# Summing the middle unit's outputs in SBUF, with one quarter of the weights' sums moved to VectorE

## The chip, the cores and the metric

The kernel runs on one core of one Trainium2 chip. The metric is the device time of one execution in microseconds; of several executions the median is given.

## The reference

Chunked attention is followed by a layer norm and a two-layer network with a residual sum:

```python
# q, k, v: (8, 8, 576, 64); chunks of 64 tokens, each attends to itself
scores = scale * q_c @ k_c.T
attn = softmax(scores)                      # the row's maximum subtracted first
x = (attn @ v_c)  -> (8, 576, 512)          # heads side by side
xn = (x - mean) / sqrt(var + 1e-6) * g_ln
out = x + max(xn @ w_ch1, 0) @ w_ch2        # 512 -> 2048 -> 512
```

The 8 x 576 = 4608 tokens are 18 pairs of 256 rows ("pair" in the code), and two pairs make a tile, so there are 9 tiles. The hidden layer of 2048 is worked on in 16 parts of 128, numbered f.

## The kernel before

**Stages.** The first three tiles (numbers 0 to 2 in the code) are computed directly, while the weights come in and are converted from 64-bit input; a matmul is done as three, from a high and a low half of each operand (`hh` and `hl` for the hidden layer, `wh` and `wl` for the weights). The third of them is called tile 3 below. The six tiles that are left form three units (u = 0, 1, 2) of two tiles, four pairs each. A unit's first product (line 1035) uses seven products in place of eight, on sums and differences of quarters of the operands; so does the second product of units 1 and 2 (line 946, class `double`). Unit 0's second product is a plain one (line 1161). Unit 1 is the middle unit, unit 2 the last one (`tail`).

**What feeds the units.** The sums of the first layer's weights (`wa`) are made by `prepare`, those of the second layer (`wb`) by `mix`, from the converted weights, on GpSimd while tile 3 is computed (`mix_early` for p = 4 to 7) and on VectorE in unit 0 (`mix_late` for p = 0 to 3); p counts eight parts of two f each. All go to DRAM and come back through a ring of six places in SBUF, which SyncE's queue fills in order (`Ring.fetch`: `wa`, `wb` and `w2d`, the plain second layer). `attention` of the next unit's pairs is woven into the running unit, at cost units that count TensorE's work (one for a matmul of 512 columns). `BEGINS[u][n]` says where pair n of the next unit begins, `PAIR_STEPS[u][n]` at which offsets its steps are played. Every pair writes its x to its rows of `out` in DRAM (`spill`, line 262) and sends a turned copy of its normalised rows to the tile `rows` (line 482). `combine` makes the operands `xc` of the next unit from `rows`, in two halves whose places are in `HALVES`: the casts are on ScalarE (line 799), the low halves on GpSimd for the first half and on VectorE for the second (line 803), and the differences on VectorE (line 806), in place, so that a difference waits for the low halves that still read the tile.

**The double product.** The seven products of line 946 are named by `DOWNS = "4126573"`. Each has eight items p, and an item is 12 matmuls of 256 columns. Items are worked on in pairs, and a pair takes one ring place. The operand of an item is split ahead of time: `high` on ScalarE (line 888) and `low` on VectorE (lines 893 and 897), into five buffers in turn, so ScalarE can write one when TensorE has left it. The functions `mix_2`, `mix_3` and `mix_4` (lines 1057, 1065 and 1062) make the next products' operands in place on VectorE. `plan` lists all of this with a due time in items, counted from the product's begin, and `advance` plays what is due behind each group of six matmuls. Two accumulator tiles of two banks each, `a` and `c`, are used in turn, each for eight items.

**What becomes of the sums.** A finished accumulator belongs to one or two quarters of the output: n is the tile of the unit, half is the half of the columns, i one of the tile's two pairs. In the last unit, x is brought back into SBUF (`bring_back`) and VectorE adds the accumulator to it (`gather`, line 911), then it is stored. In the middle unit ScalarE copies the accumulator to SBUF (`copy_out`, line 922) and GpSimd's queue issues DMAs that add the copy to the rows of `out` in DRAM (`add_out`, line 928).

**The order.** Everything is recorded under a manual schedule: each engine executes its instructions in the order in which the code issues them, and waits for what they need. What stands behind a waiting instruction on the same engine or queue waits too. The first three tiles are played from strings and tables of letters; `THIRD` is the table for tile 3: `T` and `V` are `mix_early`, `Q` is `combine`'s second half for unit 0, `H` the attention of a pair. `REST` plays the last steps of `Q` in unit 0. The tag of a tile names the memory that it takes over (`w12` was part 12 of the weights); `keep` has four buffers for x, and the pool `work` two.

Of the kernel before, what the change touches and what calls it, by code (L numbers as in the profile page):

```python
# [17 lines left out]
P = 128  # L18
# [27 lines left out]
    11: "HGGPTT", 12: "GTTT", 13: "GTT", 14: "GGHP", 15: "GHPT", 16: "GHPTT", 17: "GPTVV", 18: "HHGPVV", 19: "HGPTT",  # L46
    20: "HGPVTT", 21: "HHPVV", 22: "HPVT", 23: "TT", 24: "HT", 25: "H", 26: "QQ", 27: "QR", 28: "Q", 29: "QXXN",
    30: "QQR", 31: "Q",
# [3 lines left out]
BEGINS = ((8, 122, 236, 350), (4, 92, 152, 240))  # L52
STEPS = (0, 5, 9, 14, 20, 31, 42, 53, 61, 67, 72, 77, 85, 90, 97, 104, 111, 118, 125)
ACROSS = (0, 5, 9, 14, 20, 31, 42, 53, 61, 67, 72, 77, 110, 116, 123, 130, 136, 142, 148)
BY_TENSOR = (0, 6, 11, 18, 28, 32, 36, 44, 50, 56, 64, 69, 77, 84, 90, 96, 102)
AT_END = (0, 6, 11, 18, 28, 32, 36, 44, 50, 88, 98, 103, 110, 117, 123, 129, 135)
PAIR_STEPS = ((STEPS, STEPS, ACROSS, STEPS), (STEPS, BY_TENSOR, STEPS, AT_END))
HALVES = (((426, 8), (562, 12)), ((500, 7.5), (600, 11)))
SECOND_HALF = 528
MIXING = (1, 4, 13, 16, 24, 37, 41, 47)  # L60
# [45 lines left out]
def chunk_attention_ffn(ctx: ExitStack, tc: tile.TileContext, qkv, v01, g, w, out):  # L106
# [723 lines left out]
    class double:  # L830

        def __init__(self, u, hu, mix_2, mix_3, mix_4):
            self.hu, self.first, self.tail = hu, 2 * LEAD + 4 * u, u == UNITS - 1
            self.items = [(x, p) for x in DOWNS for p in range(NF // 2)]
            self.pools, self.split, self.ys, self.xs, self.plan = {}, {}, {}, {}, []
            for i in range(len(self.items)):
                if not self.tail:
                    at = (-5, -4.5, -1.7, -1, -0.3)[i] if i < 5 else i - 4
                elif i < 8:
                    at = (-5, -4.5, -3.5, -3, -2.5, -2, -0.9, 0.2)[i]  # L840
                else:
                    at = i - (7 if i < LONG else 6 if i < LONG + 5 else 4)
                self.plan += [(at, self.high, i), (at + 0.6, self.low, i)]
            for p in range(NF // 2):
                if self.tail:
                    self.plan += [(2.2 + 1.2 * p, mix_2, p), (13 + 1.8 * p, mix_4, p), (22 + 1.6 * p, mix_3, p)]
# [57 lines left out]
        def gather(self, bank, n, half):  # L904
            last = (n, half) == (0, 1)
            cols = slice(half * PAIR, (half + 1) * PAIR)
            for i in range(2):
                y = self.ys[bank][i].rearrange("p (j d) -> p j d", j=2)
                x = self.xs[n][:, i, :, cols]
                for j in [slice(k, k + 1) for k in range(2)] if last else [slice(0, 2)]:  # L910
                    nc.vector.tensor_tensor(out=x[:, j], in0=y[:, j], in1=x[:, j], op=ALU.add)
                    if last:
                        self.store(n, i, j.start, cols)
            if (n, half) == (0, 0) and bank == "c":
                for i in range(2):
                    for j in range(2):
                        self.store(n, i, j, cols)

        def copy_out(self, bank):
            self.staged = keep.tile([P, 2, DM], F32, name="x")  # L920
            for i in range(2):
                nc.scalar.copy(self.staged[:, i], self.ys[bank][i])

        def add_out(self, bank, places):
            for n, half in places:
                cols = slice(half * PAIR, (half + 1) * PAIR)
                for i in range(2):
                    nc.gpsimd.dma_start(
                        spilled[self.first + 2 * n + i][:, :, cols],
                        self.staged[:, i].rearrange("p (j d) -> p j d", j=2), accum_op=ALU.add,  # L930
                    )
# [67 lines left out]
    def mix_early(pool, tag, ps):  # L999
        for p in ps:  # L1000
# [3 lines left out]
                lambda k: [x[:, DM:].bitcast(F32) for x in weights(2 * p + k)], nc.gpsimd,  # L1004
# [250 lines left out]
    with tc.manual_schedule():  # L1255
# [4 lines left out]
            G=tiles[3].attention(1), H=tiles[4].attention(1, True, pt_raw=True), S=prepare(), R=start_ring(), T=mix_early(raws, "raw", (4, 5, 7)), V=mix_early(const, "w7", (6,)), P=combine(0, 0), Q=combine(0, 1),  # L1260
# [15 lines left out]
        side = [(at, now["Q"]) for at in REST]  # L1276
# [56 lines left out]
```

## Time and profile before

| | us |
|---|---|
| median of three executions | 840.89 |
| lowest and highest of them | 838.8, 842.84 |
| the profiled execution's own time | 837.73 |
| its span in the trace | 835.6 |
| TensorE busy in the span | 820.4 |
| VectorE busy | 591.5 |
| ScalarE busy | 331.5 |
| GpSimd busy | 197.7 |

All times in the trace count from the begin of the span. The stages, as TensorE's lines in the chain that ended last show them: the first three tiles until 326 us, unit 0 from 326 to about 500, unit 1's first product until 588.9 and its second until 675.2, unit 2's first until 751.4 and its second until the end. In the rows, PE is TensorE, DVE VectorE, ACT ScalarE, POOL GpSimd and SPq SyncE's queue of DMAs; L946 is line 946 of the kernel before. A timeline row gives the start, the busy time, the engine, the line, the operation, output and input by the program's names, how many instructions were merged into the row, and in brackets the idle time ahead of it and what ended it. A row of grouped instructions gives the count, the busy time, the mean of one in ns, and the idle time ahead. A row of DMA issues gives the count, the size of one, and the median time from the issue to the landing.

### The profile page before, as it was taken

What the parts mean: (1) busy time and instruction counts of PE and PEld (TensorE: products, weight loads), DVE (VectorE), ACT (ScalarE), POOL (GpSimd) and SP (SyncE); (2) the same over time, 40 slices, a digit from 0 to 9 for tenths busy, and PEclk for the clock granted to TensorE, in tenths of its full rate; (3) what the DMA queues carried; (4) which work ended last, traced back from release to release, by engine and by line L of the source; (5) the groups of instructions that cost most, each with busy time, mean ns of one, the idle gap of its engine ahead of it and who ended that gap; (6) DMA issues with size and microseconds to landing.
All of it is one profiled execution on the core that took longest, in us unless ns stands there. A gap on an engine that the chain in (4) does not pass through costs nothing.

```text
span 835.6 us, 16319 instructions
## 1 busy us (share of the span) xinstructions
PE 820.4 (98%) x6442; PEld 702.1 (84%) x6442; DVE 591.5 (71%) x959; ACT 331.5 (40%) x523; POOL 197.7 (24%) x180
## 2 busy tenths in 40 slices
PE   7999999999999999999999999999998999999998
PEld 4888888888888878888888888788998988889998
DVE  6999966787655945876787858796875932248854
ACT  4776431122322332323334443334554632255432
POOL 0110006463755893000015010000014611000000
PEclk9999999999999999999999999999999999999999
DMA  9997407948883239777867999687898898768673
GB/s 360 336 280 223 167 35 252 322 159 289 319 278 124 102 143 337 257 273 248 275 225 221 363 312 325 224 272 239 253 263 200 216 227 223 206 203 277 208 217 102
DMA packets 108092, 199.54 MB, mean 239 GB/s; under 512 B 9328, under 2 KB 66160, under 8 KB 106096
## 3 DMA queue, kind: packets, MB, share of 16 engines
q1 hardware_dynamic: 101216, 187.48, 65.8%
q0 software_dynamic: 6800, 11.01, 8.2%
q8 instruction: 51, 0.84, 0.4%
q14 instruction: 25, 0.20, 0.1%
HBM read 138.69 MB, written 50.86 MB: 227 GB/s over the span
## 4 chain that ended last, share of the span: by engine, by line
PE 87%; POOL 5%; DVE 3%; DMA 2%; ACT 1%; issue 1%; SPq 1%; DVEq 0%; POOLq 0%; ACTq 0%
PE y L1035 25%; PE y L946 19%; PE h L563 13%; PE y L587 13%; PE y L1161 8%; PE h L1161 3%; PE s L307 2%; POOL mixed L985 2%; POOL mixed L978 1%; PE h L407 1%; DMA k_t<-qkv 1%; DMA wa<-parts 1%; POOL xc L803 1%; DVE pt_sb L378 1%; PE s L407 1%
## 5 line engine op out<-in xcount | busy, mean ns | idle before, releaser
L1035 PE MATMUL y<-xc,ring 128*128 128x512 f32 x1008 | 233.7, 391 | 0.0
L1035 PEld LDWEIGHTS y<-xc,ring 128*128 128x128 f32 x1008 | 187.9, 188 | 39.5
L563 PE MATMUL h<-xth,wp 128*128 128x512 f32 (+1 forms) x432 | 129.3, 370 | 0.0
L946 PE MATMUL y<-ring,hx 128*128 128x256 f32 x876 | 110.2, 285 | 4.0 <-DVE hx L897 4.0
L946 PEld LDWEIGHTS y<-ring,hx 128*128 128x128 f32 x876 | 108.1, 194 | 4.2 <-DVE hx L897 4.2
L1044 DVE TENSOR_TENSOR hu<-y,snap 128x512 f32<-128x512 f32 x72 | 49.2, 687 | 75.5 <-ACT snap L1041 42.1
L587 PE MATMUL y<-wp,hh 128*128 128x512 f32 x376 | 96.2, 394 | 0.0
L563 PEld LDWEIGHTS h<-xth,wp 128*128 128x128 f32 x432 | 78.2, 188 | 14.1
L587 PEld LDWEIGHTS y<-wp,hh 128*128 128x128 f32 x376 | 69.1, 188 | 13.9
L563 PE MATMUL h<-xtl,wp 128*128 128x512 f32 (+1 forms) x216 | 78.2, 367 | 0.0
L577 DVE SCALAR_TENSOR_TENSOR hl<-h,hh 128x512 fp32r<-128x512 f32 (+1 forms) x53 | 33.1, 629 | 62.4 <-ACT hh L576 62.2
L1041 ACT COPY snap<-y 128x512 f32<-128x512 f32 x72 | 42.1, 586 | 80.5 <-PE y L1035 80.4
L576 ACT ACTIVATE hh<-h 128x512 fp32r<-128x512 f32 (+1 forms) x53 | 28.6, 546 | 106.2 <-PE h L563 106.2
L378 DVE STREAM_TRANSPOSE pt_sb<-p_sb 32x256 f32<-32x256 f32 x144 | 62.7, 436 | 4.6 <-ACT p_sb L342 2.3
L888 ACT ACTIVATE hx<-hu 128x512 fp32r<-128x512 f32 x73 | 45.4, 631 | 51.8 <-PE y L946 42.3
L457 POOL TENSOR_TENSOR rstd<-vare,mhalf 128x2 f32<-128x2 f32 x12 | 10.7, 891 | 192.8 <-DVE vare L456 192.8
L897 DVE TENSOR_TENSOR hx<-hu,hx 128x512 fp32r<-128x512 f32 x62 | 43.9, 718 | 12.0 <-ACT hx L888 11.3
L587 PE MATMUL y<-wp,hl 128*128 128x512 f32 x188 | 51.8, 389 | 0.0
L803 POOL TENSOR_TENSOR xc<-rows,xc 128x512 fp32r<-128x512 f32 x28 | 46.7, 1713 | 18.9 <-ACT xc L799 18.9
L563 PEld LDWEIGHTS h<-xtl,wp 128*128 128x128 f32 x216 | 40.3, 189 | 6.6 <-ACT xtl L526 0.2
L946 PE MATMUL y<-ring,hh 128*128 128x256 f32 x312 | 45.2, 283 | 0.0
L1161 PE MATMUL y<-ring,hx 128*128 128x512 f32 x162 | 42.3, 390 | 0.0
(164 smaller groups left out, 1217.8 us busy)
## 6 DMA issues: line engine op xcount, KB each, us to landing
ring<-wa SPq DMA_DIRECT2D x84, 512.0 KB, 4.7
ring<-w2d SPq DMA_DIRECT2D x32, 512.0 KB, 6.5
ring<-wb SPq DMA_DIRECT2D x32, 512.0 KB, 4.1
raw<-w SPq DMA_DIRECT2D x15, 1024.0 KB, 6.9
ring<-w2d SPq DMA_DIRECT2D x48, 256.0 KB, 3.9
q_t<-qkv SPq DMA_DIRECT2D x17, 512.0 KB, 4.7
k_t<-qkv SPq DMA_DIRECT2D x17, 512.0 KB, 6.9
v_t<-qkv SPq DMA_DIRECT2D x32, 256.0 KB, 6.6
```

Of the source, the lines that this page charges most:

```text
L378: nc.vector.transpose(out=pt_sb[quad(2 * h2 + j), :, c, quad(i)], in_=p_sb[quad(2 * c + i), :, h2, quad(j)])
L563: nc.tensor.matmul(h, lhsT=(wh, wh, wl)[m][:, ks], rhs=(xth, xtl, xth)[m][:, k, :], start=i == 0, stop=i == len(terms) - 1,)
L577: nc.vector.scalar_tensor_tensor(out=hl, in0=h, scalar=0.0, in1=hh.bitcast(F32), op0=ALU.max, op1=ALU.subtract)
L587: nc.tensor.matmul(sums(pairs[j // 2])[j % 2], lhsT=(hh, hh, hl)[m], rhs=(wh, wl, wh)[m], start=f == 0 and m == 0, stop=f == NF - 1 and m ...
L803: engine.tensor_tensor(out=o[:, 1], in0=x, in1=o[:, 0].bitcast(F32), op=ALU.subtract)
L888: nc.scalar.activation(hh, self.split[i][2], AF.Relu if x == "1" else AF.Copy)
L897: nc.vector.tensor_tensor(out=hl, in0=x, in1=hh.bitcast(F32), op=ALU.subtract)
L946: nc.tensor.matmul(bank[j // 2][:, j % 2 * PAIR : (j % 2 + 1) * PAIR], lhsT=(hh, hh, hl)[m][:, j * P : (j + 1) * P], rhs=loaded[t // 2][:, ...
L1035: nc.tensor.matmul(bank, lhsT=w[:, (0, 0, 1)[m], ks], rhs=x[:, (0, 1, 0)[m], k, :], start=start and k == m == 0, stop=k == 1 and m == 2, s ...
L1041: nc.scalar.copy(out, bank)
L1044: nc.vector.tensor_tensor(out=out, in0=bank, in1=s, op=ALU.add)
L1161: nc.tensor.matmul(ys[j], lhsT=(hh, hh, hl)[m], rhs=w[:, (0, 1, 0)[m]], start=f == 0 and m == 0, stop=f == NF - 1 and m == 2,)
```

## The change

In the middle unit the copies and the adding DMAs go, but for two accumulators. x of the four pairs is brought into SBUF by four loads (`bring_pair`), VectorE adds five of the accumulators from PSUM (`gather`, now for both units, six sums of two instructions), and four stores write the rows (`store_pair`). The first two accumulators (after products 4 and 1) end before x is there: ScalarE copies them into buffers of `work` (`stage`), and VectorE adds the copies later (`add_staged`). A `gather` has a due time 1.5 to 2.5 items behind the accumulator's end. `mix_2` and `mix_4` of the middle unit get other due times.

Of the weights' sums that GpSimd made during tile 3, part 7 goes to VectorE: it starts with the last tokens of tile 3 (`W`) and ends in unit 0 at cost units 8 to 28 (`LAST_MIXED`).

In unit 1 the steps of the next unit's pairs are respaced: the second pair's transposes come five cost units later, the third pair begins at 154 instead of 152 and has wider steps in its first half, and the fourth begins at 246 instead of 240, with its later steps at the same places as before.

```diff
 THIRD = {
-    ... 19: "HGPTT", 20: "HGPVTT", 22: "HPVT", 23: "TT", 24: "HT", 29: "QXXN", 30: "QQR", 31: "Q",
+    ... 19: "HGP", 20: "HGPV", 22: "HPV", 24: "H", 29: "QXXNWW", 30: "QQRW", 31: "QW",
-BEGINS = ((8, 122, 236, 350), (4, 92, 152, 240))
+BEGINS = ((8, 122, 236, 350), (4, 92, 154, 246))
 STEPS = (0, 5, 9, 14, 20, 31, 42, 53, 61, 67, 72, 77, 85, 90, 97, 104, 111, 118, 125)
-BY_TENSOR = (0, 6, 11, 18, 28, 32, 36, 44, 50, 56, 64, 69, 77, 84, 90, 96, 102)
-AT_END = (0, 6, 11, 18, 28, 32, 36, 44, 50, 88, 98, 103, 110, 117, 123, 129, 135)
-PAIR_STEPS = ((STEPS, STEPS, ACROSS, STEPS), (STEPS, BY_TENSOR, STEPS, AT_END))
+BY_TENSOR = (0, 6, 11, 18, 33, 37, 40, 48, 54, 60, 67, 72, 80, 87, 93, 99, 105)
+WIDE = (0, 5, 9, 14, 22, 35, 48, 61, 69, 75, 80, 85, 93, 98, 105, 112, 118, 124, 130)
+AT_END = (0, 6, 11, 18, 33, 37, 40, 48, 54, 82, 92, 97, 104, 111, 117, 123, 129)
+PAIR_STEPS = ((STEPS, STEPS, ACROSS, STEPS), (STEPS, BY_TENSOR, WIDE, AT_END))
+LAST_MIXED = (8, 16, 21, 28)
...
                 else:
-                    self.plan += [(6 + 1.6 * p, mix_2, p), (14.5 + 1.7 * p, mix_4, p), (27 + 1.4 * p, mix_3, p)]
+                    self.plan += [(5.2 + 1.5 * p, mix_2, p), (16 + 1.3 * p, mix_4, p), (27 + 1.4 * p, mix_3, p)]
             if self.tail:
                 self.plan += [(0, self.bring_back, 1), (4, self.bring_back, 0)]
+            else:
+                self.plan += [(at, self.bring_pair, n, i) for at, n, i in ((6, 0, 0), (9, 0, 1), (12, 1, 0), (15, 1, 1))]
             for at, bank, *places in (
                 (8, "c", (1, 0)), (16, "a", (0, 0)), (24, "c", (0, 0)), (32, "a", (0, 1)), (40, "c", (1, 1)),
                 (48, "a", (1, 1), (1, 0)), (56, "c", (0, 1)),
             ):
+                if not self.tail and at < 24:
+                    self.plan += [
+                        (at + 0.5, self.stage, bank, at), (28.5 if at == 16 else 37.5, self.add_staged, at, *places[0])
+                    ]
+                    continue
+                for k, place in enumerate(places):
+                    late = 0 if self.tail or at == 56 else 1.5 + k if at == 48 else 2.5
+                    self.plan.append((at + late, self.gather, bank, *place))
+            for i in range(2):
                 if self.tail:
-                    self.plan += [(at, self.gather, bank, *place) for place in places]
+                    self.plan += [(49 + i, self.store, 1, i, j) for j in range(2)]
                 else:
-                    self.plan += [(at, self.copy_out, bank), (at, self.add_out, bank, places)]
-            if self.tail:
-                self.plan += [(49 + i, self.store, 1, i, j) for i in range(2) for j in range(2)]
+                    self.plan += [(51.5 + i, self.store_pair, 1, i), (56, self.store_pair, 0, i)]
...
         def gather(self, bank, n, half):
-                x = self.xs[n][:, i, :, cols]
+                x = self.xs[n][:, i, :, cols] if self.tail else self.xs[n][i][:, :, cols]
...
-        def copy_out(self, bank):
-            self.staged = keep.tile([P, 2, DM], F32, name="x")
+        def stage(self, bank, at):
+            self.staged[at] = work.tile([P, 2, DM], F32, name="xg", tag="work")
             for i in range(2):
-                nc.scalar.copy(self.staged[:, i], self.ys[bank][i])
+                nc.scalar.copy(self.staged[at][:, i], self.ys[bank][i])
-        def add_out(self, bank, places):
-            for n, half in places:
-                cols = slice(half * PAIR, (half + 1) * PAIR)
-                for i in range(2):
-                    nc.gpsimd.dma_start(
-                        spilled[self.first + 2 * n + i][:, :, cols],
-                        self.staged[:, i].rearrange("p (j d) -> p j d", j=2), accum_op=ALU.add,
-                    )
+        def add_staged(self, at, n, half):
+            for i in range(2):
+                x = self.xs[n][i][:, :, half * PAIR : (half + 1) * PAIR]
+                y = self.staged[at][:, i].rearrange("p (j d) -> p j d", j=2)
+                nc.vector.tensor_tensor(out=x, in0=y, in1=x, op=ALU.add)
+        def bring_pair(self, n, i):
+            if n not in self.xs:
+                self.xs[n] = [None] * 2
+            self.xs[n][i] = unspill(self.first + 2 * n + i)
+        def store_pair(self, n, i):
+            nc.sync.dma_start(spilled[self.first + 2 * n + i], self.xs[n][i])
...
-    def mix_early(pool, tag, ps):
+    def mix_early(pool, tag, ps, engine):
...
-T=mix_early(raws, "raw", (4, 5, 7)), V=mix_early(const, "w7", (6,))
+T=mix_early(raws, "raw", (4, 5), nc.gpsimd), V=mix_early(const, "w7", (6,), nc.gpsimd), W=mix_early(const, "w12", (7,), nc.vector)
...
-        side = [(at, now["Q"]) for at in REST]
+        side = [(at, now["Q"]) for at in REST] + [(at, now["W"]) for at in LAST_MIXED]
```

More of the change, by code (lines that the diff above doesn't have):

```diff
@@ L45 @@
     0: "CS", 1: "CS", 2: "DDGS", 3: "DS", 4: "DDS", 5: "DS", 6: "DGS", 7: "GGHSTT", 8: "DGTT", 9: "D", 10: "GGPT",
-    11: "HGGPTT", 12: "GTTT", 13: "GTT", 14: "GGHP", 15: "GHPT", 16: "GHPTT", 17: "GPTVV", 18: "HHGPVV", 19: "HGPTT",
-    20: "HGPVTT", 21: "HHPVV", 22: "HPVT", 23: "TT", 24: "HT", 25: "H", 26: "QQ", 27: "QR", 28: "Q", 29: "QXXN",
-    30: "QQR", 31: "Q",
+    11: "HGGPTT", 12: "GTTT", 13: "GTT", 14: "GGHP", 15: "GHPT", 16: "GHPTT", 17: "GPTVV", 18: "HHGPVV", 19: "HGP",
+    20: "HGPV", 21: "HHPVV", 22: "HPV", 24: "H", 25: "H", 26: "QQ", 27: "QR", 28: "Q", 29: "QXXNWW", 30: "QQRW",
+    31: "QW",
 }
 ROOMS = {1: (3, 9), 2: (6,)}
-BEGINS = ((8, 122, 236, 350), (4, 92, 152, 240))
+BEGINS = ((8, 122, 236, 350), (4, 92, 154, 246))
 STEPS = (0, 5, 9, 14, 20, 31, 42, 53, 61, 67, 72, 77, 85, 90, 97, 104, 111, 118, 125)
 ACROSS = (0, 5, 9, 14, 20, 31, 42, 53, 61, 67, 72, 77, 110, 116, 123, 130, 136, 142, 148)
-BY_TENSOR = (0, 6, 11, 18, 28, 32, 36, 44, 50, 56, 64, 69, 77, 84, 90, 96, 102)
-AT_END = (0, 6, 11, 18, 28, 32, 36, 44, 50, 88, 98, 103, 110, 117, 123, 129, 135)
-PAIR_STEPS = ((STEPS, STEPS, ACROSS, STEPS), (STEPS, BY_TENSOR, STEPS, AT_END))
+BY_TENSOR = (0, 6, 11, 18, 33, 37, 40, 48, 54, 60, 67, 72, 80, 87, 93, 99, 105)
+WIDE = (0, 5, 9, 14, 22, 35, 48, 61, 69, 75, 80, 85, 93, 98, 105, 112, 118, 124, 130)
+AT_END = (0, 6, 11, 18, 33, 37, 40, 48, 54, 82, 92, 97, 104, 111, 117, 123, 129)
+PAIR_STEPS = ((STEPS, STEPS, ACROSS, STEPS), (STEPS, BY_TENSOR, WIDE, AT_END))
 HALVES = (((426, 8), (562, 12)), ((500, 7.5), (600, 11)))
 SECOND_HALF = 528
+LAST_MIXED = (8, 16, 21, 28)
 MIXING = (1, 4, 13, 16, 24, 37, 41, 47)
@@ L833, in __init__ @@
             self.hu, self.first, self.tail = hu, 2 * LEAD + 4 * u, u == UNITS - 1
+            self.staged = {}
             self.items = [(x, p) for x in DOWNS for p in range(NF // 2)]
@@ L904, in gather @@
         def gather(self, bank, n, half):
-            last = (n, half) == (0, 1)
+            last = self.tail and (n, half) == (0, 1)
             cols = slice(half * PAIR, (half + 1) * PAIR)
@@ L913, in gather @@
                         self.store(n, i, j.start, cols)
-            if (n, half) == (0, 0) and bank == "c":
+            if self.tail and (n, half) == (0, 0) and bank == "c":
                 for i in range(2):
@@ L1003, in mix_early @@
                 p, t_[:, 0], t_[:, 1].bitcast(F32R),
-                lambda k: [x[:, DM:].bitcast(F32) for x in weights(2 * p + k)], nc.gpsimd,
+                lambda k: [x[:, DM:].bitcast(F32) for x in weights(2 * p + k)], engine,
             )
@@ L1259, in chunk_attention_ffn @@
             A=now.pop("E"), B=tiles[2].attention(1), C=tiles[3].attention(0, True), D=tiles[4].attention(0, True),
-            G=tiles[3].attention(1), H=tiles[4].attention(1, True, pt_raw=True), S=prepare(), R=start_ring(), T=mix_early(raws, "raw", (4, 5, 7)), V=mix_early(const, "w7", (6,)), P=combine(0, 0), Q=combine(0, 1),
+            G=tiles[3].attention(1), H=tiles[4].attention(1, True, pt_raw=True), S=prepare(), R=start_ring(), T=mix_early(raws, "raw", (4, 5), nc.gpsimd), V=mix_early(const, "w7", (6,), nc.gpsimd), W=mix_early(const, "w12", (7,), nc.vector), P=combine(0, 0), Q=combine(0, 1),
         )
```

## Prediction

> **What bounds the kernel now.** I read the page's first part, then TensorE's waits, then the chain that ended last, then the timeline around each wait of TensorE.
>
> ```profile
> PE 820.4 (98%) x6442; PEld 702.1 (84%) x6442; DVE 591.5 (71%) x959; ACT 331.5 (40%) x523; POOL 197.7 (24%) x180
> ...
> PE y L946 <- DVE hx L897: 4.0, 1, 4.0
> ...
> PE s L495 <- ACT xg L469: 1.0, 1, 1.0
> ...
> PE s L366 <- ACT p_sb L342: 0.2, 1, 0.2
> ...
> 588.90 45.61 PE y L946 x380
> ...
> 641.33 33.83 PE y L946 x268
> 675.16 76.19 PE y L1035 x336
> 751.35 80.64 PE y L946 x672
> ```
>
> TensorE is busy for 820.4 us of a span of 835.6, so only its waits can be won, unless an engine beside it becomes slower than it. The list of its waits (us in total, times, longest) has one of 4.0 us at L946, one of 1.0 at L495 and one of 0.2 at L366 away from the start. The chain shows that the first costs more than itself. The 672 matmuls of L946 of the last unit take 80.64 us in one piece, 0.120 us each. Those of the middle unit start at 588.90, run 380 at the same pace (45.61), and the last 268 end at 641.33 + 33.83 = 675.16: 86.26 us in all, 5.6 more. What this wait hangs on:
>
> ```profile
> 629.31 0.60 ACT L799 CAST xc<-rows 128x512 fp32r<-128x512 f32 x1
> 630.22 0.63 ACT L888 ACTIVATE hx<-hu 128x512 fp32r<-128x512 f32 x1 [0.30 <-PE y L946]
> ...
> 635.18 1.21 POOL L928 DMA_DIRECT2D out<-x  x1 [4.90 <-ACT hh L888]
> 635.94 4.18 POOL L803 TENSOR_TENSOR xc<-rows,xc 128x512 fp32r<-128x512 f32 x3
> ...
> 638.94 1.73 DVE L806 TENSOR_TENSOR rows<-rows 128x512 f32<-128x512 f32 x1 [8.81 <-POOL xc L803]
> ...
> 641.33 3.61 PE L946 MATMUL y<-ring,hx 128*128 128x256 f32 x16 [3.96 <-DVE hx L897]
> ```
>
> A row of the combining on VectorE (L806) sits for 8.81 us until GpSimd has done its L803, which reads the same tile. GpSimd starts L803 only at 635.94, since six accumulating DMAs of the middle unit (L928) stand ahead in its queue and each waits for data or for an earlier one (4.90 us before the sixth). Behind L806 on VectorE stands the low half (L897) that TensorE needs. ACT wrote its high half at 630.22 + 0.63, so without the block it would have been done at about 631.5; TensorE ran dry at 641.33 - 3.96 = 637.37. **A delay of 5.8 us on VectorE is thus free, and only what exceeds it is lost.** When TensorE returns, 16 matmuls take 3.61 us, 0.226 us each, 0.106 more than usual: 1.7 us. Together 4.0 + 1.7 agree with the 5.6 read from the chain.
>
> **The change, part by part.**
>
> *The accumulating DMAs go.* 16 issues of L928 leave GpSimd, and its seven L803 of the middle unit follow their casts at once (the third cast starts at 629.31, while the sixth DMA still waits at 635.18). The block of 8.81 us goes, and with it 5.6 us. What is late next is either VectorE by itself or the ring, so both are counted.
>
> *VectorE gets the sums.* Ten of the 14 copies leave ACT; 16 additions of 128x512 come to VectorE, twelve reading PSUM and four reading two SBUF tiles. On VectorE, in the middle unit where the combining's first half begins, before (L897 the low halves, L1065 the mixing, L806 the combining):
>
> ```order
> L897 TENSOR_TENSOR hx<-hu,hx 128x512
> L1062 TENSOR_TENSOR hu<-hu 128x512
> L897 TENSOR_TENSOR hl<-hu,hh 128x512
> L1065 TENSOR_TENSOR hu<-hu 128x512
> L897 TENSOR_TENSOR hl<-hu,hh 128x512
> L1065 TENSOR_TENSOR hu<-hu 128x512
> L897 TENSOR_TENSOR hx<-hu,hx 128x512
> L806 TENSOR_TENSOR rows<-rows 128x2x8x32
> ```
>
> The same place now (L909 low halves, L1082 mixing, L923 the sum from PSUM, L940 from the staged copy, L808 combining):
>
> ```order
> L909 TENSOR_TENSOR hx<-hu,hx 128x512
> L923 TENSOR_TENSOR x<-y,x 128x2x256 x2
> L909 TENSOR_TENSOR hl<-hu,hh 128x512
> L1082 TENSOR_TENSOR hu<-hu 128x512
> L909 TENSOR_TENSOR hl<-hu,hh 128x512
> L1082 TENSOR_TENSOR hu<-hu 128x512
> L940 TENSOR_TENSOR x<-xg,x 128x2x256 x2
> L909 TENSOR_TENSOR hx<-hu,hx 128x512
> L808 TENSOR_TENSOR rows<-rows 128x2x8x32
> ```
>
> Four additions now stand between the low halves ahead of the first combining row. Their price:
>
> ```profile
> 651.43 1.88 DVE L897 TENSOR_TENSOR hx<-hu,hx 128x512 fp32r<-128x512 f32 x3
> 653.90 1.12 DVE L897 TENSOR_TENSOR hl<-hu,hh 128x512 fp32r<-128x512 f32 x1 [0.58 <-ACT hh L888]
> 655.23 1.49 DVE L897 TENSOR_TENSOR hl<-hu,hh 128x512 fp32r<-128x512 f32 x1 [0.20 <-ACT hh L888]
> 656.64 1.77 DVE L803 TENSOR_TENSOR xc<-rows,xc 128x512 fp32r<-128x512 f32 x1
> ...
> 663.87 3.28 DVE L897 TENSOR_TENSOR hx<-hu,hx 128x512 fp32r<-128x512 f32 x2
> ...
> 316.42 1.29 POOL L803 TENSOR_TENSOR xc<-rows,xc 128x512 fp32r<-128x512 f32 x1 [2.90 <-ACT xc L799]
> ...
> 646.11 11.76 POOL L803 TENSOR_TENSOR xc<-rows,xc 128x512 fp32r<-128x512 f32 x3
> ...
> L911 DVE TENSOR_TENSOR back<-y,back 128x512 f32<-128x512 f32 x12 | 7.6, 686 | 5.2 <-PE y L946 5.2
> ```
>
> Three low halves take 1.88 us, so one follows another every 0.60 us; an addition from PSUM (the last unit has them, 686 ns) is of that length. In the densest stretch, 15 items of 12 matmuls (15 x 12 x 0.120 = 21.6 us of TensorE), VectorE had 28 rows and now has 35: 35 x 0.60 = 21.0 us, so it just keeps pace. GpSimd comes on top. Beside its three L803 from 646.11 VectorE's rows grow from 0.69 to 1.12, 1.49 and 1.77 (2.3 us together), two rows at 663.87 take 3.28 in place of 1.28 (2.0), and the one at 638.94 takes 1.73 (1.0): 5.3 us for seven L803, all of which now fall into the dense stretch or just behind it. Backlog: 5.3 - 0.6 = 4.7 us, under the free 5.8. Lower bound of the loss 0; upper bound, if each L803 held VectorE for its whole length (1.29 alone, at 316.42) and one more were waited for by L808: 7 x 1.29 + 1.3 - 0.6 - 5.8 = 3.9 us. I take 0.5, near the measured growth. The banks are not at risk before that: a bank is written again eight items after its last product (11.5 us), and its reader starts 2.5 items (3.6 us) in.
>
> The Trainium skill's page "SBUF — State Buffer" speaks against this part in the section on the shared port pair: a VectorE instruction with two SBUF inputs and a GpSimd instruction that reads SBUF exclude each other, and the loser waits for the whole instruction. By that rule the upper bound of 3.9 us is the loss and not 0.5, and rival 1 below the outcome, for the low halves, the mixing and L940 have two SBUF inputs; the sums from PSUM would not be held. The trace agrees in kind and not in size: VectorE's rows grew by 5.3 us in place of 9.0, and from 646.11 it was GpSimd that waited (11.76 us for three).
>
> *The partial results come in through SP's queue.* Four loads of 512 KB (L268) are put among the ring's loads, four stores behind. SP before, around the middle unit's first items (L482 the turned rows, L723 and L725 the ring):
>
> ```order
> L723 DMA ring<-w2d 128x2x256 x2
> L482 DMA rows<-x 32x2x128 x8
> L723 DMA ring<-w2d 128x2x256 x2
> L482 DMA rows<-x 32x2x128 x4
> L723 DMA ring<-w2d 128x2x256 x6
> L725 DMA ring<-wb 128x4x256 x12
> ```
>
> And now (L484 the turned rows, L725 and L727 the ring):
>
> ```order
> L725 DMA ring<-w2d 128x2x256 x2
> L268 DMA x<-out 128x2x512
> L484 DMA rows<-x 32x2x128 x4
> L725 DMA ring<-w2d 128x2x256 x2
> L268 DMA x<-out 128x2x512
> L725 DMA ring<-w2d 128x2x256 x4
> L268 DMA x<-out 128x2x512
> L727 DMA ring<-wb 128x4x256
> L268 DMA x<-out 128x2x512
> L727 DMA ring<-wb 128x4x256 x11
> ```
>
> One load now stands ahead of the unit's ring place 9 (counted from 0), two ahead of 10 and 11, three ahead of 12, four ahead of 13.
>
> ```profile
> 606.94 2.62 SPq L482 DMA_DIRECT2D rows<-x  x4
> 609.66 3.86 SPq L723 DMA_DIRECT2D ring<-w2d  x6
> 613.61 21.76 SPq L725 DMA_DIRECT2D ring<-wb  x10
> ...
> ring<-w2d SPq DMA_DIRECT2D x2, 256.0 KB, 3.5
> ...
> ring<-w2d SPq DMA_DIRECT2D x2, 256.0 KB, 3.9
> ...
> ring<-wb SPq DMA_DIRECT2D x3, 512.0 KB, 9.0
> ...
> q0 software_dynamic: 365, 0.36, 44.5%
> q1 hardware_dynamic: 928, 0.68, 40.8%
> ```
>
> Here SP issues without a pause, some 0.64 us for each DMA, and the ring runs late. A place feeds 24 matmuls, 2.88 us. Place 9 was issued at 609.66 and 610.30, landed 3.5 us later (613.8), and is used from 588.90 + 9 x 2.88 = 614.8: a margin of 1.0 us. Place 10 has 617.7 - (609.66 + 3 x 0.64 + 3.9) = 2.2. Place 12 was issued behind the six, at 613.6; with the 9.0 us of its neighbours it lands at 622.6 and is used at 623.5: 0.9. The loads ahead add 0.64 us each in issue, and bytes: the hardware queue took 40.8% of 6 us for 0.68 MB, 3.6 us for a MB, so 1.9 for 512 KB. The accumulating DMAs that go took 44.5% for 0.36 MB, 7.4 us for a MB, 1.9 for each 256 KB. So place 9 keeps 0.4; place 12 gets 3 x 0.64 = 1.9 of issue, and the bytes about cancel: 1.0 late. If they don't cancel, 2 x 1.9 more, 4.8 late. Bounds 0 and 4.8; I take 0.8, as the accumulating DMAs that go lie in the same stretch (the row of the software queue is from there). The stores wait for VectorE at the unit's end with five ring places loaded ahead, 5 x 12 x 0.227 = 13.6 us at the next unit's pace (336 matmuls in 76.19): nothing.
>
> *One quarter of the weights' sums moves from GpSimd to VectorE at tile 3's end.* The rows:
>
> ```profile
> 297.71 3.97 POOL L985 TENSOR_TENSOR mixed<-mixed 128x256 f32<-128x256 f32 x4
> 298.24 0.23 DVE L456 TENSOR_SCALAR vare<-mv 128x2 f32<-128x2 f32 x1
> ...
> 301.64 0.70 POOL L457 TENSOR_TENSOR rstd<-vare,mhalf 128x2 f32<-128x2 f32 x1
> ...
> 303.15 0.66 PE L495 MATMUL s<-ident,xg 128*128 128x128 f32 x4 [0.99 <-ACT xg L469]
> ...
> 316.47 2.57 DVE L806 TENSOR_TENSOR rows<-rows 128x512 f32<-128x512 f32 x2
> ...
> 319.61 0.59 ACT L576 ACTIVATE last<-h 128x512 fp32r<-128x512 f32 x1
> 320.23 0.69 DVE L577 SCALAR_TENSOR_TENSOR last<-h,last 128x512 fp32r<-128x512 f32 x1 [1.18 <-ACT last L576]
> 321.16 0.84 PE L587 MATMUL y<-wp,last 128*128 128x512 f32 x3
> ...
> L985 DVE TENSOR_TENSOR hu<-hu 128x256 f32<-128x256 f32 x16 | 6.8, 423 | 0.4
> ```
>
> The wait of 1.0 us at L495 came from here: rstd (L457) had its input at 298.24 + 0.23, but stood behind four sums of this quarter (L985) until 301.64. These go, so rstd comes some 3 us earlier, and the 1.0 us with it. In exchange VectorE gets at tile 3's end (L806 and L808 combining, L577 and L579 the last low half):
>
> ```order
> L806 TENSOR_TENSOR rows<-rows 128x2x2x128 x2
> L577 SCALAR_TENSOR_TENSOR last<-h,last 128x512
> L595 TENSOR_SCALAR vare<-mv 128x2 x2
> L605 SCALAR_TENSOR_TENSOR x<-y,rstd,x 128x512 x4
> ```
>
> now:
>
> ```order
> L808 TENSOR_TENSOR rows<-rows 128x2x2x128
> L995 TENSOR_TENSOR mixed<-wp 128x512 x2
> L808 TENSOR_TENSOR rows<-rows 128x2x2x128
> L1002 TENSOR_TENSOR mixed<-mixed 128x256 x2
> L579 SCALAR_TENSOR_TENSOR last<-h,last 128x512
> L597 TENSOR_SCALAR vare<-mv 128x2 x2
> L1002 TENSOR_TENSOR mixed<-mixed 128x256 x2
> L607 SCALAR_TENSOR_TENSOR x<-y,rstd,x 128x512 x4
> ```
>
> Four sums stand ahead of the last low half: 2 x 0.60 + 2 x 0.42 = 2.0 us. The combining rows ended at 319.04, so VectorE is at it at 321.0 in place of 320.23 and done at 321.7; TensorE uses it third in the group at 321.16, so at 321.6. ACT's half stands behind a cast that needs the second L808, 1.2 us later: 321.4 in place of 320.2, wanted at 321.16. Loss between 0 (if GpSimd's earlier queue brings the combining forward) and 2.0; I take 0.5, the two small lags together. The sums behind (two of 0.42) fit ahead of L607, which waits for TensorE and for rstd. The two last rows, in the first unit, are 1.2 us on VectorE beside a TensorE that never waits there.
>
> *Pair steps respaced.* The same rows are spread; ACT's exponent gets 5 matmuls (5 x 0.227 = 1.1 us) more ahead of VectorE and the transposes, and L366's wait of 0.2 us goes.
>
> **Sum.** 5.6 + 1.0 + 0.2 = 6.8 won; 0.5 + 0.8 + 0.5 = 1.8 given back; 5.0 net. The profiled execution took 837.73 us (span 835.6), so 832.7. It stands 3.2 us under the median of the runs shown, 840.89; against that median 835.9.
>
> **Rivals.** (1) VectorE becomes the bound of the middle unit: the upper bound of 3.9 in place of 0.5. For it: 35 rows in 21.6 us and GpSimd beside them. Against: TensorE's own waits slow the demand, and the growth measured was smaller. 835.9 + 3.4 = 839.3. (2) The ring is late: 4.8 in place of 0.8 gives 839.9, 3.0 gives 838.1. For it: margins of about 1 us. Against: the ten loads behind (613.61) take 21.76 us, 2.2 us each, so SP waits for TensorE again and the lag is passing. (3) Slower: a load L268 that waits for its buffer (a turned tile still being sent out by L484) holds SP, and every ring load behind it. To end 0.5% above 840.89 all 6.8 must go and 4.2 more, 11 us: 1.7 of it from the slow clock after a long wait, so 9.3 of waiting above the margin of 1.0, a hold of some 10 us; below 1.0 it costs nothing. The turned rows stand ahead in the same queue and SP's issue of four takes 2.62 us, so a hold of 3 to 4 us is the most that I see. (4) The change leaves the wait where it is, since L808 still waits for L803: for it, that GpSimd can starve beside a full VectorE (11.76 us for three); the price is a part of rival 1.
>
> **How the numbers follow.** About 0.5% (4.2 us) is what a measurement of this kernel can tell from no change: 836.7 and below is faster. The forecast, with losses below 2.6 in all, 0.57; rival 1 with 4, 0.17; rival 2, 0.18, both mostly within 0.5%; rival 3, 0.08. The range goes from 834.1 (no loss at all) less 1.1 for the spread of the runs (838.8 to 842.84) to 840.0, which takes in rivals 1 and 2.
>
> **What the profile would show.** L928 gone; L803 of the middle unit at 626 to 650; L808 without a wait of more than 2 us; TensorE's waits at L495 and at the middle unit's L946 gone. Rival 1: a wait of TensorE for L909 around 640 to 650. Rival 2: a wait for the ring's DMA at 614 to 627. Tile 3: a wait of TensorE for "last" at about 321. If TensorE's busy time with the same matmuls is more than 820 us, or the waits return elsewhere, the forecast is wrong.

## The result, and the profile after

Five executions of the changed kernel have a median of 834.15 us (833.33 to 835.8), five of the kernel before, beside them on the same chip, 840.07 us (838.8 to 842.84). The ratio is 0.9929 with a 95% interval of 0.9907 to 0.9951, 5.9 us less; the forecast was 5.0 less. The profiled execution of after took 835.8 us (span 834.0), the longest of its five; that of before took 837.73 and lies below all five of its own. The two traces by themselves thus show only 1.9 us, and what is compared below is the stages.

The page's first line on the engines, the queues, and TensorE's waits for the middle unit and for the rows of tile 3, after:

```profile
PE 821.6 (99%) x6442; PEld 701.5 (84%) x6442; DVE 601.5 (72%) x983; ACT 326.7 (39%) x513; POOL 174.3 (21%) x156
...
q0 software_dynamic: 2448, 6.82, 4.4%
...
PE y L963 <- DMA ring<-w2d: 2.3, 2, 1.2
...
PE y L1052 <- DMA ring<-wa: 0.4, 1, 0.4
...
PE h L565 <- DVE hl L579: 0.2, 1, 0.2
```

VectorE has 10 us more work and GpSimd 23 us less. The wait of 4.0 us for VectorE's low half is gone, and so are those at tile 3's rows (1.0) and at the scores (0.2). In their place stands one for the ring: 2.3 us in two pieces.

The chain that ended last, after:

```profile
317.77 8.67 PE y L589 x36
...
589.82 2.87 PE y L963 x24
592.74 23.24 PE y L963 x192
615.98 5.25 DMA ring<-w2d
621.36 52.16 PE y L963 x432
673.52 76.19 PE y L1052 x336
749.71 80.64 PE y L963 x672
```

The middle unit's second product goes from 589.82 to 673.52, 83.70 us, where it took 86.26. The 672 matmuls of the last unit still show what it takes without a wait, 80.64, so 3.1 us are left in it. The same stretch in a table by stages, the row of before first and that of after behind it (length, then busy time and instructions of TensorE, its weight loads, VectorE, ScalarE and GpSimd, the granted clock, the DMA engines' share and GB/s):

```profile
588.90:675.16 86.26, 82.30 (x674) 82.10 (x673) 65.53 (x95) 46.92 (x82) 30.40 (x19) 0.98 0.88 232
...
589.82:673.52 83.70, 81.39 (x674) 80.83 (x673) 72.38 (x109) 43.59 (x74) 22.09 (x8) 1.00 0.78 247
```

The clock in this stage rises from 0.98 to 1.00, and the DMA engines' share falls from 0.88 to 0.78 while they move more a second. Where the 3.1 us lie, on TensorE's timeline:

```profile
617.06 3.11 PE L963 MATMUL y<-ring,hx 128*128 128x256 f32 x24 [1.07 <-DMA ring<-w2d]
621.36 1.19 PE L963 MATMUL y<-ring,hh 128*128 128x256 f32 x8 [1.19 <-DMA ring<-w2d]
```

These are the ring's places 9 (behind 24 + 192 matmuls, 24 to a place) and 10, 2.3 us of waiting in all; the rest of the 3.1 is made of small lags around and between them. After both, the matmuls go on at about the usual pace, 24 in 3.11 us. And the two engines that the prediction argued about, GpSimd and then VectorE, where the combining begins:

```profile
629.62 1.30 POOL L805 TENSOR_TENSOR xc<-rows,xc 128x512 fp32r<-128x512 f32 x1 [39.14 <-DMA ring<-wb]
632.59 3.57 POOL L805 TENSOR_TENSOR xc<-rows,xc 128x512 fp32r<-128x512 f32 x2 [1.67 <-DMA ring<-wb]
642.86 16.56 POOL L805 TENSOR_TENSOR xc<-rows,xc 128x512 fp32r<-128x512 f32 x4 [6.70 <-ACT xc L801]
...
633.23 3.48 DVE L940 TENSOR_TENSOR x<-xg,x 128x512 f32<-128x512 f32 x2
636.63 0.68 DVE L909 TENSOR_TENSOR hx<-hu,hx 128x512 fp32r<-128x512 f32 x1
637.24 0.68 DVE L808 TENSOR_TENSOR rows<-rows 128x512 f32<-128x512 f32 x1
...
644.46 1.27 DVE L923 TENSOR_TENSOR x<-y,x 128x512 f32<-128x512 f32 x2
...
650.47 0.67 DVE L909 TENSOR_TENSOR hl<-hu,hh 128x512 fp32r<-128x512 f32 x1
...
653.48 1.27 DVE L923 TENSOR_TENSOR x<-y,x 128x512 f32<-128x512 f32 x2
...
655.88 2.38 DVE L909 TENSOR_TENSOR hx<-hu,hx 128x512 fp32r<-128x512 f32 x2
658.19 1.78 DVE L805 TENSOR_TENSOR xc<-rows,xc 128x512 fp32r<-128x512 f32 x1
```

GpSimd now starts its low halves at 629.62 (it was 635.94), and VectorE's first combining row at 637.24 has no idle time ahead of it, where it had 8.81 us. VectorE is late all the same, at most at 650.47. That row is the low half of item 41, the tenth from the one at 636.63, which is item 32; its high half is due when TensorE begins item 37. TensorE begins item 20 (240 matmuls) at 621.36 and takes 1.44 us for each, so it is at item 37 at 645.8, and with 0.6 for ScalarE's half the low half could have run at 646.4. It is 4.1 us late, below the 5.8 us that are free, and TensorE waits nowhere for it. The two rows of L923, which add a sum out of PSUM, are taken up in the last section.

### The profile page after: what moved, and what is told of

Its sections match the earlier page's. It is cut to its first block, busy times and chain, and to the rows that moved or that the text cites. A ratio compares the mean times of both kernels' runs of the same rounds, so it can differ in the third digit from the quotient of the medians.

```text
span 834.0 us, 16308 instructions
## 1 busy us (share of the span) xinstructions
PE 821.6 (99%) x6442; PEld 701.5 (84%) x6442; DVE 601.5 (72%) x983; ACT 326.7 (39%) x513; POOL 174.3 (21%) x156
## 4 chain that ended last, share of the span: by engine, by line
PE 90%; DMA 5%; SPq 2%; DVE 1%; ACT 1%; issue 1%; DVEq 0%
PE y L1052 25%; PE y L963 19%; PE h L565 15%; PE y L589 15%; PE y L1178 7%; PE h L1178 2%; PE s L309 2%; DMA ring<-wa 2%; PE h L409 1%; DMA ring<-w2d 1%; DMA wp<-wf 1%; SPq L484 1%; DMA k_t<-qkv 1%; PE s L409 1%; PE s L358 1%
## 5 line engine op out<-in xcount | busy, mean ns | idle before, releaser
L805 POOL TENSOR_TENSOR xc<-rows,xc 128x512 fp32r<-128x512 f32 x28 | 50.4, 1811 | 71.0 <-DMA ring<-wb 40.8
```

Source lines behind the costliest of these rows:

```text
L805: engine.tensor_tensor(out=o[:, 1], in0=x, in1=o[:, 0].bitcast(F32), op=ALU.subtract)
```

## The experiments

All were compared with the kernel before on the same chip. Both versions were run again first, and the change was cut in two: its sums in the middle unit alone, and all the rest alone. In `mid_only` the code of the class `double` is that of after and everything else is of before; in `rest_only` it is the other way round.

**Before and after again.**

> The kernel before once more, unchanged, for its spread. If the profiled execution of before was an ordinary one, the middle unit's second product takes 86.3 us again (672 matmuls, 80.64 in the last unit), with one wait of TensorE of about 4 us behind the combining, and the ratio is 1.000. If that wait varies from one execution to the next, the product's time differs from 86.3 by more than 1 us.

> The changed kernel once more. The median gain was 5.9 us, but the two profiled executions differ by 1.9 only. If the profiled execution of after was a late one, the ring's waits of 2.3 us in the middle unit are smaller here (0 to 1.5 us), and the profiled execution stands 4 to 6 us under that of before on this chip. If the ring's waits belong to the change, they are 2 us or more again.

Before gave 840.78 us, 1.0009 [0.9995, 1.0023] of the other executions of the same kernel. After gave 835.12, 0.9942 [0.9923, 0.9961]. Its profiled execution took 836.99 us and that of before 839.65: 2.7 apart, again less than the medians; 4 to 6 had been expected in case the first trace of after was a late one. In the second trace of before the wait was longer:

```profile
PE y L946 <- DVE hx L897: 5.2, 1, 5.2
...
643.20 34.22 PE y L946 x268
677.41 76.19 PE y L1035 x336
```

The second product took about 87.9 us there, and in the second trace of after 84.21, with a wait for the ring of 2.9, so this wait belongs to the change. What a product without a wait would save is thus 5.6 us in one execution of before and 7.3 in the other. The wait of 1.0 us at tile 3's rows was 0.3 in this second trace of before.

**The sums in the middle unit alone.**

```diff
 # double as in the changed kernel; all else as before
-THIRD, BEGINS, BY_TENSOR, AT_END, PAIR_STEPS, mix_early and side of after
+THIRD, BEGINS, BY_TENSOR, AT_END, PAIR_STEPS, mix_early and side of before
```

> Before with the middle unit's sums in SBUF alone: the quarter of the weights' sums stays on GpSimd, the pair steps stay. My theory (the adding DMAs ahead of the low halves in GpSimd's queue made the wait): the middle unit's second product falls from 86.3 to 81 to 84 us, TensorE keeps the wait of 1.0 us at tile 3 for xg, and the time is 2.5 to 5.5 us under before. Rival (the respacing made the room): the product stays above 85 us.

834.31 us, 0.9934 [0.992, 0.9948]: 5.8 us under before, a little more than expected. Its wait for the ring, the begin of its second product in the chain, and the begin of what follows:

```profile
PE y L961 <- DMA ring<-w2d: 0.9, 1, 0.9
...
590.96 22.93 PE y L961 x192
...
672.70 76.19 PE y L1050 x336
```

The product takes 81.74 us. No wait of TensorE for VectorE's low half is left in it, although GpSimd still makes the low halves of the combining. The wait at tile 3's rows was 0.3 us, not 1.0.

**The rest alone: the moved quarter and the respaced steps.**

> The moved quarter and the respaced steps, with the adding DMAs left as before. My theory: the middle unit's second product stays at about 86 us with the 4 us wait, the 1.0 us wait at tile 3 goes and 0.5 us comes back there, so the time is 0 to 1 us under before. Rival (tile 3 or the respacing bring the gain): 3 us or more under before.

839.03 us, 0.9993 [0.9978, 1.0007]: nothing that can be measured. The old wait stands in its trace, and the second product takes 87.66 us:

```profile
PE y L948 <- DVE hx L899: 4.5, 1, 4.5
...
588.33 45.71 PE y L948 x380
...
675.99 76.19 PE y L1037 x336
```

Within what these times can tell, the whole gain of the change is the middle unit's sums.

**The wait without the adding DMAs' removal.** The prediction put the wait down to GpSimd's order: low halves behind DMAs that wait. Here the DMAs stay as they were, and only those low halves go to VectorE:

```diff
-        engine = nc.vector if u > 0 and half == 1 else nc.gpsimd
+        engine = nc.vector if u > 0 and half == 1 or u == 2 else nc.gpsimd
```

> Before, with one word changed: the seven low halves of the combining's first half in the middle unit are made on VectorE in place of GpSimd; the adding DMAs all stay. My theory (the wait came from the low halves standing behind the adding DMAs in GpSimd's order, not from the DMAs' traffic or from the copies): VectorE gets 7 x 0.60 = 4.2 us more and loses the 8.8 us block; the product of the middle unit falls from 86.3 to 88 us to 80.6 to 82, and the time is 4 to 6.5 us under before. Rival (the traffic of the adding DMAs or VectorE's load holds TensorE): 85 us or more, no change in time.

832.93 us, 0.9914 [0.9893, 0.9935], 7.4 us under before, where 4 to 6.5 had been expected. A timeline of GpSimd and VectorE, and the chain:

```profile
632.56 1.22 POOL L928 DMA_DIRECT2D out<-x  x1 [7.25 <-ACT hx L888]
...
638.16 1.21 POOL L928 DMA_DIRECT2D out<-x  x1 [4.38 <-ACT hh L888]
...
631.81 0.68 DVE L803 TENSOR_TENSOR xc<-rows,xc 128x512 fp32r<-128x512 f32 x1
...
633.62 0.68 DVE L806 TENSOR_TENSOR rows<-rows 128x512 f32<-128x512 f32 x1
...
591.74 80.63 PE y L946 x672
```

GpSimd still sits for 7.25 and 4.38 us between its DMAs, but nobody waits for it any more, and the product runs in one piece. So the adding DMAs alone do not make the wait, and by `mid_only`, where GpSimd still makes the low halves, those alone do not either. It takes both in one order on GpSimd; the transfers themselves cost this product nothing. One changed expression does what the whole change does, and the seven rows that VectorE gets are 0.60 us apart, 4.2 us in all, about what GpSimd's seven cost VectorE in after.

**How much VectorE may be late.** After, with eight more rows of 128x512 on VectorE at item 30.2 (each takes x's maximum with itself, which leaves x as it is):

```diff
+            if not self.tail:
+                self.plan += [(30.2, self.again)] * 8
+        def again(self):
+            x = self.xs[0][0][:, :, :PAIR]
+            nc.vector.tensor_tensor(out=x, in0=x, in1=x, op=ALU.max)
```

> The changed kernel with eight more VectorE instructions of 128x512 (a maximum of x with itself, which leaves x as it is) at 30.2 items of the middle unit's second product, 8 x 0.60 = 4.8 us. The prediction's claim is that VectorE may run 5.8 us late before TensorE waits. In the changed kernel's trace its low halves run 3.3 us late at item 32 and at most 4.2 at item 41. So with 4.8 more the lateness is 8 to 9 us, and TensorE waits for VectorE by 2.2 to 3.2 us; the time is 1 to 3.5 us above the changed kernel's. Rival (VectorE has no such margin and each row costs its length): 4.8 us or more above. Rival (the margin is larger): no wait, same time.

837.72 us, 0.9973 [0.9955, 0.9991]. TensorE's waits, its timeline and VectorE's:

```profile
PE y L969 <- DVE hx L911: 2.7, 1, 2.7
...
646.02 0.95 PE L969 MATMUL y<-ring,hx 128*128 128x256 f32 x4 [2.75 <-DVE hx L911]
646.77 1.91 PE L969 MATMUL y<-ring,hh 128*128 128x256 f32 x8
...
639.61 5.76 DVE L946 TENSOR_TENSOR x<-x 128x512 f32<-128x512 f32 x8
```

TensorE waits 2.7 us for the low half, where the free 5.8 us leave 4.1 + 8 x 0.60 - 5.8 = 3.1. It then runs slowly for a while, a matmul in 0.24 us in place of 0.12; a wait of 1.7 us for the ring is in this trace as well, as in after's. The time lies 3.6 and 2.6 us above the two medians of after. So the margin is real, after uses most of it, and by these numbers rival 1 begins some three rows further on.

**The loads of x from another queue.** The first reading of the new wait was that the loads stand ahead of the ring in SyncE's queue. They were put into GpSimd's, in after and in `mid_only`:

```diff
-        nc.sync.dma_start(x, spilled[pair])
+        queue.dma_start(x, spilled[pair])          # nc.gpsimd for bring_pair
```

> The changed kernel with the four loads of x issued from GpSimd's queue in place of SyncE's. My theory (the loads push the ring's loads back in SyncE's queue): TensorE's waits for the ring, 2.3 and 2.9 us in two executions of the changed kernel, fall to 0 to 0.8, the product of the middle unit from 83.7 and 84.2 to 80.7 to 82, and the time to 1 to 3 us under the changed kernel's. Rival (the respaced pair steps push SyncE's turned rows later, the loads matter little; the middle unit alone had a wait of 0.9): waits of 1.5 us or more stay.

> Only the middle unit's sums (no moved quarter, no respacing), and their loads from GpSimd's queue. Both theories of the ring's lateness give no ring wait in the middle unit here: 80.6 to 81.2 us for its product, and a time 0.5 to 1.5 us under that of the middle unit's sums alone (834.31 on that chip, ratio 0.9934), so about 0.992.

833.8 us, 0.9931 [0.9907, 0.9955], and 835.79, 0.9943 [0.9921, 0.9965]: misses. The waits for the ring stay, 2.3 us in the first, as its rival had it, and 2.0 in the second, which neither theory had and where `mid_only` had 0.9. The loads' places in the queue are not the whole cause. In the second (GpSimd's loads, then TensorE):

```profile
615.09 0.72 POOL L266 DMA_DIRECT2D x<-out  x1 [14.52 <-PE y L961]
...
622.80 1.46 PE L961 MATMUL y<-ring,hh 128*128 128x256 f32 x8 [1.97 <-DMA ring<-w2d]
```

Here the matmuls wait for the second half of place 10, which SyncE issued as the fourth of a row from 612.87, at about 614.8: it needed 8 us to land, with 512 KB of x issued beside it at 615.09.

**Early loads or respaced steps.** Two causes were left: the loads' bytes beside the ring, and the respaced pairs, whose turned rows (L484) SyncE issues ahead of the ring. Three runs, each against after or `mid_only`: the loads later, in both; and after with the tables of before.

```diff
-((6, 0, 0), (9, 0, 1), (12, 1, 0), (15, 1, 1))
+((17, 0, 0), (18.5, 0, 1), (20, 1, 0), (21.5, 1, 1))      # late_loads, late_loads_mid
```

```diff
-BEGINS, BY_TENSOR, WIDE, AT_END, PAIR_STEPS of after       # mid_quarter
+BEGINS, BY_TENSOR, AT_END, PAIR_STEPS of before
```

> The changed kernel with the four loads of x (L268) due at items 17, 18.5, 20 and 21.5 instead of 6, 9, 12 and 15, so that they stand behind the ring's places 9 to 13 in SyncE's queue. Theory A, the bytes of the loads and their place ahead of the ring make the ring late: TensorE's waits at L963 for the ring fall from 2.3 to 2.9 us to under 0.8, and the middle unit's second product from 83.7 or 84.2 to about 81.5 us; the time falls by some 1 to 2 us, to about 832.5. Rival B, the respaced pairs send their turned rows (L484) later and these hold the ring: the wait stays at 2 us or more, the product at 83 to 84 us, the time at about 834.

> The kernel before with the middle unit's sums alone (as mid_only), and the four loads at items 17 to 21.5 instead of 6 to 15. Both theories: no or hardly a wait for the ring (it was 0.9 us with the early loads), the second product 80.7 to 81.2 us instead of 81.74; the time 833 to 834.3, the same as mid_only within its interval or up to 1 us less. A wait of TensorE for VectorE's low half would show that the sums now wait for x.

> The changed kernel without the respacing: the pairs' tables of before, with the sums in the middle unit and the moved quarter. Theory A: the wait for the ring is as in the changed kernel, 2 us or more, since the loads stand where they stood. Rival B, the respacing is what makes the ring late: the wait is 0 to 1 us, as in mid_only (0.9), and the turned rows (x8 in SyncE's queue) are issued about 10.6 us behind the begin of the product instead of 13. The time: 834 by A, 833 to 834 by B; the comparison of the times can hardly tell them apart, the waits can.

`late_loads` 832.47 us, 0.9912 [0.9887, 0.9937]; `late_loads_mid` 833.38, 0.9918 [0.9894, 0.9942]; `mid_quarter` 833.73, 0.9924 [0.99, 0.9948]. The times do not tell these three apart; their waits differ. `late_loads` and its chain:

```profile
PE y L963 <- DMA ring<-wb: 0.5, 1, 0.5
...
591.61 78.16 PE y L963 x648
669.77 76.19 PE y L1052 x336
```

then `late_loads_mid` and `mid_quarter`:

```profile
588.81 80.63 PE y L961 x672
```

```profile
590.88 80.63 PE y L962 x672
```

Later loads take the wait for `w2d` away with the respacing in place, as theory A had it; what is left in `late_loads` is a wait for place 1 at 591.61, long before the loads are issued. In `mid_quarter` the old spacing takes it away with the early loads in place, as rival B had it. Over all the traces, no kernel without early loads waits for `w2d` in this product, respaced (`rest_only`, `late_loads`) or not. With early loads the waits are 1.7 to 2.9 us in the respaced kernels, and 0, 0.9 and 2.0 in those with the old spacing (`mid_quarter`, `mid_only`, `mid_loads_gpsimd`). So the early loads are needed for the wait; that the respacing lengthens it rests on one trace of most kernels. SyncE's timeline of `mid_quarter` and of after shows how it can: the turned rows, and the two loads of place 9 behind them.

```profile
601.43 5.77 SPq L483 DMA_DIRECT2D rows<-x  x8
...
611.94 1.24 SPq L724 DMA_DIRECT2D ring<-w2d  x2
```

```profile
602.81 5.90 SPq L484 DMA_DIRECT2D rows<-x  x8
...
613.45 1.24 SPq L725 DMA_DIRECT2D ring<-w2d  x2
615.98 2.48 SPq L725 DMA_DIRECT2D ring<-w2d  x4
```

Counted from the second product's begin in the chain (590.88 and 589.82), the turned rows go out at 10.6 us in `mid_quarter` and at 13.0 in after, and place 9 at 21.1 and 23.6. It is used at 9 x 2.88 = 25.9, and a landing of 3.5 us makes 24.6 and 27.1. The second is 1.2 late, and 1.07 was waited. Before issued it at 20.8 (609.66 - 588.90). `mid_quarter`, which has one load ahead of it and not the respacing, is only 0.3 later, and `late_loads`, which has the respacing and no load ahead, was at 22.6 and did not wait. Place 10 lies behind a second load and waited 1.19 more; that this is the load's doing is argued from `late_loads`, where the load is not there and the wait neither. The places in the queue do not settle everything. `mid_loads_gpsimd` sent its turned rows out at 12.3 us with the old spacing, and `mid_only` and `mid_quarter` issued place 10 alike, 22.9 and 23.0 us behind the begin, and only the first waited (0.9). How long a landing takes varies too, and why is open.

| kernel | us | ratio | interval | wait of the second product |
|---|---|---|---|---|
| `rest_only` | 839.03 | 0.9993 | 0.9978 to 1.0007 | low half 4.5 |
| `eight_more_rows` | 837.72 | 0.9973 | 0.9955 to 0.9991 | low half 2.7, ring 1.7 |
| `mid_loads_gpsimd` | 835.79 | 0.9943 | 0.9921 to 0.9965 | ring 2.0 |
| after, again | 835.12 | 0.9942 | 0.9923 to 0.9961 | ring 2.9 |
| `mid_only` | 834.31 | 0.9934 | 0.992 to 0.9948 | ring 0.9 |
| after | 834.15 | 0.9929 | 0.9907 to 0.9951 | ring 2.3 |
| `loads_on_gpsimd` | 833.8 | 0.9931 | 0.9907 to 0.9955 | ring 2.3 |
| `mid_quarter` | 833.73 | 0.9924 | 0.99 to 0.9948 | none |
| `late_loads_mid` | 833.38 | 0.9918 | 0.9894 to 0.9942 | none |
| `low_on_vector` | 832.93 | 0.9914 | 0.9893 to 0.9935 | none |
| `late_loads` | 832.47 | 0.9912 | 0.9887 to 0.9937 | ring 0.5 |

The lowest of them, `late_loads`, is a version that beats before and has a lower median than after; but its interval overlaps that of after, and so do those of all the versions below `eight_more_rows` in the table. That it is 2 us better than after is not shown by the times; in the two traces its second product is 2.2 us shorter (81.5 against 83.70).

## Why the prediction was right, and where its steps were off

**The sign, the size and the mechanism of the gain held.** 835.9 was forecast with 833.0 to 840.0, and 834.15 came. The first term, 5.6 us for a wait that hangs on GpSimd's order, is confirmed from two sides: `mid_only` has the whole gain, and `low_on_vector` gets it with the DMAs still there. Of the signs that the prediction named, the old wait and L928 went and L808 had no wait of more than 2 us in the middle unit; GpSimd's low halves ran on until 659, not 650. Two signs against it came as well: the wait for the ring of rival 2, and a busy time of TensorE above 820 us (821.6). The second was no sign to go by, since before's own 820.4 is above it.

**VectorE's lateness, taken as 0.5 (bounds 0 to 3.9), was 0.** The free 5.8 us were read rightly. The backlog came near in size, 4.1 in the trace for the 4.7 worked out, but not in what it is made of. VectorE's rows grew by 2.2 us at 633.23 (3.48 for two, against 1.27 for two at their usual pace), 1.1 at 655.88 and 1.1 at 658.19, 4.4 for the seven low halves of GpSimd, where 5.3 had been taken from before. Only the first 2.2 lie ahead of 650.47, where the backlog was longest; the rest of the 4.1, by difference, is VectorE's own rows, the sums among them. So the nearness of 4.7 and 4.1 is in part luck. Rival 1 did not come, nor rival 4, since L808 waits for nothing in the middle unit. The rule of the Trainium skill's page "SBUF — State Buffer" (section "SBUF: two separate sides", the exclusive shared pair) would have given 3.9 us of loss. The trace agrees that one engine can shut the other out, since four low halves, one of which took 1.30 us at 629.62, took 16.56 on GpSimd from 642.86, while VectorE's rows beside them kept their 0.60 us until 655.88; it was mostly GpSimd that lost, and TensorE waited for neither.

**The ring's lateness, taken as 0.8 (bounds 0 to 4.8), was 3.1 us, the one term that was clearly mis-sized.** The bounds held, the step did not. It gave place 9 a margin of 0.4 and saw the risk at place 12; the waits came at places 9 and 10, and 12 was in time. What the step lacked is, as far as these traces show, the respacing and longer landings: of the pairs' moved steps the prediction counted ScalarE's and VectorE's room and put the rest at nothing, though each pair's turned rows are DMAs in SyncE's queue ahead of the ring. They went out 2.4 us later than in `mid_quarter` (in `rest_only`, without the loads, 1.3 later than in before), and the loads came on top. "The bytes about cancel" does not hold either, by the landings from 605 to 622 us: a ring load of 256 KB landed in 3.5 us in before (the median of eight) and in 4.6 in after. It was 4.6 in `rest_only` too, so how much of this is the loads' own is open.

**The end of tile 3, taken as 0.5, was 0.51** (the chain's row at 317.77, 8.67 against 8.16 before). The 1.0 us at L495 did go, since rstd no longer stands behind the quarter's sums on GpSimd and runs as soon as its input is there (a row of after's timeline):

```profile
299.27 1.13 POOL L459 TENSOR_TENSOR rstd<-vare,mhalf 128x2 f32<-128x2 f32 x1 [4.13 <-DVE vare L458]
```

But the wait was only 0.3 in the second trace of before, and over the six traces that keep this quarter on GpSimd it lies between 0.3 and 1.0 (1.0 again in `late_loads_mid`). The part of the change that removes it gave no time that can be measured (`rest_only`). So 1.0 was the upper end of what it costs. The 0.2 at L366 went, and is back with the old spacing in `mid_quarter`; it is too small to be seen in a time.

**Rival 3, a load that holds SyncE's queue for 10 us, did not come**: each load's row of issue is about half a microsecond.

**The sum.** With the ring's 3.1 and VectorE's 0 in it, the sum is 6.8 - 3.6 = 3.2 us, not 5.0; the ring's lateness is rival 2 at its 3.0, for which the prediction gave 838.1. The traces go with the smaller sum: the second product gained 2.56 us between the first two and 3.7 between the second two, and the profiled executions 1.9 and 2.7. The medians gained 5.9 and 5.0. So the time came out nearer to the forecast than its terms did.

Part of the gap is on record. Before's wait varies, and the granted clock of an execution goes with it: 0.998 in the trace with a wait of 4.0 us, 0.996 in those with 4.5 (`rest_only`) and 5.2. Of the 65 executions of before that were timed with the experiments, 41 had a clock of 0.996 or less and a median of 841.1 us, and 23 had 0.998 and a median of 838.95. The first profiled execution of before, from which 5.6 was read, is thus of the shorter and rarer kind. For the commoner kind the second trace of before gives 7.3 in its place, and the sum would be 4.9: an estimate, from one trace of each kind. By it, the first term and the ring's were each too small by about 2 us, and the two errors offset. That is luck. Why both profiled executions of after lie above its median is open: the traces show only profiled executions. The stretch from the begin of unit 0 to the second product varies from 262.3 to 264.8 us between them, before's and after's lying among each other, and it goes with no step of the change.

## What to carry to other kernels

A wait in front of the busiest engine can be one of order, not of work, as here: look first at what stands behind a waiting instruction in a queue, and try the smallest edit that takes the late piece out of that queue. Here one changed expression did what four new functions and two tables did. When steps are moved, follow every DMA that they issue through its queue and ask which later loads it is now ahead of; and before a wait's length is put into a sum, read it in a second execution. A time inside the forecast does not show that the terms were right: compare them one by one.

## What was not expected of the hardware

Beside a full VectorE, GpSimd nearly stood still: four rows took 16.56 us (17.75 in the second trace of after), and VectorE lost nothing beside them for the first 13 us. The first two of the four ended at about 645.7 and 654.7, each at the end of a pair of sums that VectorE reads out of PSUM (L923 at 644.46 and 653.48); the row between them took 9.06 us, and the pair of L940 at 649.27, with both inputs in SBUF, did not end it. The second trace has the same picture (rows ending at about 647.0 and 655.9, L923 at 645.71 and 654.74), and the low half of 1.30 us at 629.62 ran beside such a pair as well. With VectorE's losses elsewhere, 4.4 us for seven rows, GpSimd's help was worth nothing here: on VectorE itself the seven take 4.2 us (`low_on_vector`).

TensorE's pace after a wait changed within a narrow range of lengths. In the second products it went on at full pace after 1.07, 1.19, 1.71 (`eight_more_rows`, for the ring) and, in the second trace of after, 1.79 us. After 1.97 (`mid_loads_gpsimd`) and 2.75 us (`eight_more_rows`) the first matmuls took 0.18 to 0.24 us in place of 0.12, and the granted clock was 0.61 from 622.80 to 626 and 0.57 from 646 to 650. The Trainium skill's page "TensorE: Matmul & The Clock Gate" (section "What's actually happening") puts the fall of the clock behind an idle window of about 3.4 us; the two shorter waits here were slowed all the same.
